# Plain float32 instead of a split for the y steps of the second token tile of batch 0

## The chip, the cores and the metric

One Trainium2 chip, one core. The metric is the device time of one launch in microseconds (us): lower is better. The kernel before takes 1445.43 us (median of three runs, 1445.27 to 1445.69).

## The reference, cut to what matters

```python
p_packed = sm_attn(p, k, v)                 # 32 packed queries read all 576 keys
out = sm_attn(q, p_packed, p_packed)        # every query reads the 32 packed rows
x = out.transpose(0, 2, 1, 3).reshape(4608, 512)
h = x @ w_in                                # first MLP, 512 -> 2048
g = where(h >= 1, h, where(h <= -1, 0, (h + 1)**2 / 4))
y = g @ w_out                               # 2048 -> 512
h2 = y @ w2_in
return (h2 * sigmoid(h2)) @ w2_out          # second MLP
```

There are 8 batches of 576 tokens. Everything is float32.

## The kernel before, in words

The kernel runs attention and the first MLP batch by batch, then the second MLP over all tokens. The change lies in the first MLP of batch 0, within the first 140 us of the program.

**Steps.** A batch has 576 tokens, in two token tiles t = 0 and 1 of 288, and the 2048 hidden features are 16 blocks m of 128. A step is one tile and one block. Batch 0 runs in four groups of eight: steps 0 to 7 are tile 0 with blocks 0 to 7, steps 8 to 15 tile 1 with blocks 0 to 7, steps 16 to 23 tile 0 with blocks 8 to 15, steps 24 to 31 tile 1 with blocks 8 to 15. From batch 1 on a tile runs through all 16 blocks.

**What a step does.** `a_h` (L652, matmuls L661) computes the 128 x 288 block of h: six matmuls into one of the four banks of `ps_h`. `a_relu` (L671) makes u = (relu(h/2 + 1/2)) squared on ACT, two instructions (L676, L677). `a_max` (L680, DVE L682) finishes u and frees the bank. Then a split step makes g, a pair of fp32r numbers: `a_hi` (ACT cast, L686) rounds u, `a_lo` (L689, L692) subtracts. `a_y` (L694) multiplies g by the block's output weights into four accumulators of `ps_a`, one for each 128 columns of y: for each, three fp32r matmuls (high x high, high x low, low x high; L707), so twelve in a step. A plain step has no g: `a_y` multiplies u by plain float32 weights, one matmul for each accumulator (L703), which the trace records as two. `plain(s)` (L668) says which steps these are: before, steps 0 to 7.

**Low parts.** `a_lo` runs on POOL for blocks 0 to 7 of batch 0 and on DVE elsewhere. At the end of each group of eight, ACT and DVE copy the four accumulators to `ysb` (L716, L719), or DVE adds them to what is there (L714), and the next group's first y step may overwrite an accumulator only when it has been copied.

**Weights.** The weights arrive as float64 words. `conv_a` (ACT, L147) and `conv_b` (two DVE instructions, L153 and L154) turn a block into float32. `conv_c` (L191) splits it: ACT casts the high part (L194) and POOL subtracts (L196). Blocks 0 to 7 are kept plain for steps 0 to 7 and split for steps 8 to 15 and later batches.

**Buffers.** `big` has 37 buffers of 4 KB per partition. u has two homes: plain steps take one of the four buffers of tag `g`, which g tiles take too, all others one of three buffers of tag `u`. The buffer of a u is free when its last reader is through: the low part for a split step, the y matmuls for a plain one.

**Order.** All engines work through their own queue in program order. The queue's order is that of numbers: each job has a key, by default worked out from the step it belongs to (`hi`, `lo`, `co` and so on at the end of the function), and a table `START` by hand gives the key of most jobs of batch 0: relu17 (the relu of step 17) has 13.81, y13 14.6, relu19 15.373, y15 16.603, lo17 16.632. Jobs are sorted by key once; a job that needs something later simply waits in its queue. Besides the steps, the queues hold batch 1's attention (`front`, `back8`) and the products `wp` of packed rows with input weights (`wp_out`, L136 and L137).

Of the kernel before, what the change touches and what calls it, by code (L numbers as in the profile page):

```python
# [8 lines left out]
F32 = mybir.dt.float32  # L9
# [4 lines left out]
ALU = mybir.AluOpType  # L14
# [58 lines left out]
def attention_then_two_mlps(ctx: ExitStack, tc: tile.TileContext, kT, vv, qT, pT, w_in, w_out, w2_in, w2_out, out):  # L73


    nc = tc.nc
    B, P, NJ, S = kT.shape
# [7 lines left out]
    KF = DFF // P  # L85
# [4 lines left out]
    FW = 512  # L90
# [11 lines left out]
    big = ctx.enter_context(tc.tile_pool(name="big", bufs=37))  # L102
# [46 lines left out]
    def to_f32_end(dst, raw):  # L149


        words = words_of(raw)
        nc.vector.tensor_single_scalar(words[:, :, 0], words[:, :, 0], 29, op=ALU.logical_shift_right)  # L153
        nc.vector.scalar_tensor_tensor(  # L154
            dst.bitcast(U32), words[:, :, 1], 3, words[:, :, 0], op0=ALU.logical_shift_left, op1=ALU.bitwise_or
        )

    raw_t, part_t, w_t = {}, {}, {}
# [23 lines left out]

    def conv_b(key):
        if key[0] == "o" and key[1] < KF // 2:
            w = big.tile([P, FW], F32, tag="big", name="w")
        else:
            w = cv.tile([P, FW], F32, tag="w", name="w")
        to_f32_end(w, raw_t.pop(key))
        w_t[key] = w
# [459 lines left out]
    h_ps, u_t, g_t, acc, y_t = {}, {}, {}, {}, {}  # L649
# [16 lines left out]


    def plain(s):  # L668
        return s[:2] == (0, 0) and s[2] < KF // 2

    def a_relu(s):  # L671
        if plain(s):
            u = wk.tile([P, HB], F32, tag="g", name="u", bufs=4)
        else:
            u = a2_p.tile([P, HB], F32, tag="u", name="u", bufs=3)
        nc.scalar.activation(u, h_ps[s][:, :HB], AF.Relu, bias=half, scale=0.5)  # L676
        nc.scalar.activation(u, u, AF.Square)  # L677
        u_t[s] = u
# [9 lines left out]

    def a_lo(s):  # L689
        g = g_t[s]  # L690
        eng = nc.gpsimd if s[0] == 0 and s[2] < KF // 2 else nc.vector
        eng.tensor_tensor(g[:, 1], u_t.pop(s), g[:, 0].bitcast(F32), op=ALU.subtract)  # L692

    def a_y(s):  # L694
        b, t, m = s
        first, last = m in starts[b], m + 1 in starts[b] or m == KF - 1
        if first:
            acc["y"] = [ps_a.tile([P, 512], F32, tag="acc", name="ps_y") for _ in range(KD)]
        w = w_t["o", m]
        g = u_t.pop(s) if plain(s) else g_t.pop(s)  # L700
        for d in range(KD):
            if plain(s):
                nc.tensor.matmul(  # L703
                    acc["y"][d][:, :HB], w[:, d * P:(d + 1) * P], g, start=first, stop=last
                )
            for n, (i, k) in enumerate(() if plain(s) else PASSES):
                nc.tensor.matmul(  # L707
                    acc["y"][d][:, :HB], w[:, i, d * P:(d + 1) * P], g[:, k],
                    start=(first and n == 0), stop=(last and n == 2),
                )  # L710
            if last:
                if ("y", d // 2) in part_t:
                    ysb = part_t["y", d // 2]
                    nc.vector.tensor_tensor(ysb[:, d % 2], acc["y"][d][:, :HB], ysb[:, d % 2], op=ALU.add)  # L714
                elif d % 2:
                    nc.scalar.copy(ysb[:, 1], acc["y"][d][:, :HB])  # L716
                else:
                    ysb = wk.tile([P, 2, HB], F32, tag="ysb", name="ysb", bufs=2)
                    nc.vector.tensor_copy(ysb[:, 0], acc["y"][d][:, :HB])  # L719
                if d % 2:  # L720
                    part_t.pop(("y", d // 2), None)
                    nc.sync.dma_start(y_dram[:, d - 1:d + 1, t, b * HB:(b + 1) * HB], ysb)
# [226 lines left out]
    def ev(key, fn, *args):  # L949
        events.append((key, len(events), fn, args))  # L950
# [4 lines left out]
    def job(name, key, fn, *args):  # L955
        ev(START.get(name, key), fn, *args)
# [6 lines left out]
    with tc.manual_schedule():  # L963
# [36 lines left out]
        def c(letter, key):  # L1000
            if letter == "a":
                seq("a" + kn(key), conv_a, key)
            elif letter == "b":
                seq("b" + kn(key), conv_in if key[0] == "in" else conv_b, key)
            else:
                seq("c" + kn(key), conv_c, key)
# [56 lines left out]
        for i in (2, 3):  # L1063
            for k in range(6):
                job(f"S{i}.{k}", -2 + k + 0.6, s2j[i][k][0])
        job("bo2", -LA + 0.62, conv_b, ("o", 2))
        job("ao3", -LA + 1.62, conv_a, ("o", 3))
        job("bo3", -LA + 2.62, conv_b, ("o", 3))
        T_F1 = -1
        for i, key in enumerate(ins[KD:2 * KD]):  # L1070
# [16 lines left out]
        for m in range(4, KF):  # L1087
            n = m - 3 if m < KF // 2 else m + G['oraw'] + 1
            key = ("o", m)
# [3 lines left out]
            if m >= KF // 2:  # L1093
                job(f"co{m}", n + 2 + .66, conv_c, key)
        for m in range(KF // 2):
            job(f"co{m}", KF // 2 + m - 2.4, conv_c, ("o", m))
        job("part0", 2 * KF // 2 + KF // 2 - 5 + .67, load_part, 0, 0)
        job("part1", 2 * KF - 5 + .67, load_part, 0, 1)

# [41 lines left out]
        for p in range(NPR):  # L1141
            for kind, n in (("i2", G['ai'] + G['ad'] * p), ("o2", G['ai'] + G['ad'] * p + 12)):
                for x in range(2):
                    key = (kind, 2 * p + x)
# [59 lines left out]
        for i, (kind, step) in enumerate(steps):  # L1204
            if kind == "a":
                h = late.get(i, i - LA)
                hi = min(h + 2, i - 1)
                lo = min(h + 3, i - 1)
                if i < 20:
                    job(f"h{i}", h + 0.3, a_h, step)  # L1210
                    job(f"relu{i}", h + 1 + 0.31, a_relu, step)
                    if not plain(step):
                        job(f"hi{i}", hi + (0.32 if hi > h + 1 else 0.35), a_hi, step)
                        job(f"lo{i}", lo + (0.33 if lo > hi else 0.36), a_lo, step)
                    job(f"max{i}", h + 1 + 0.34, a_max, step)
                    job(f"y{i}", i + 0.9, a_y, step)
                else:
                    when(h, 0, a_h, step)
                    when(h + 1, 1, a_relu, step)
                    when(hi, 2 if hi > h + 1 else 5, a_hi, step)  # L1220
                    when(lo, 3 if lo > hi else 6, a_lo, step)
                    when(h + 1, 4, a_max, step)
                    when(i, 9, a_y, step)
# [42 lines left out]
```

## Time and profile before

| what | value |
|---|---|
| median of three runs | 1445.43 us |
| the profiled execution | 1445.66 us |
| its span, first to last instruction | 1443.6 us |
| PE busy | 1429.9 us, 99% of the span |
| DVE, ACT, POOL busy | 951.3, 766.2 and 74.8 us |
| granted TensorE clock | full in all 40 slices |
| PE on the chain that ended last | 90% |
| DVE on it | 5% |

PE is TensorE's matmuls, DVE VectorE, ACT ScalarE, POOL GpSimd. In a timeline row stand the start in us from the span's start, the time that the merged instructions took, engine, line, operation, tiles, shapes and count, and in brackets idle time before the row with what ended it. The time of a matmul row overlaps the next row, so a step's cost is read as the distance between starts. The line numbers are those of the kernel before.

### The profile page before, as it was taken

The page shows a single profiled execution, that of the slowest core. Times are in us where ns is not written, and L with a number is a line of the kernel's source. Part 1 is how long each engine was busy: PE and PEld are TensorE (multiplying, and loading weights), DVE is VectorE, ACT ScalarE, POOL GpSimd, SP SyncE. Part 2 cuts the span into 40 slices and gives each one's busy share as a digit, 9 for nine tenths or more (in the row PEclk, how much of TensorE's full clock was granted, in tenths as well). Part 3 has the DMA queues.
Part 4 walks back from the last instruction along what each step waited for, and adds up shares of the span by engine and source line. Part 5 has one row for each costly group of instructions (what it writes and reads, how often), then busy time and mean ns, then how long its engine had stood idle before and what let it go on. Part 6 is the DMA issues. An engine that isn't in the chain of part 4 may idle for free.

```text
span 1443.6 us, 26352 instructions
## 1 busy us (share of the span) xinstructions
PE 1429.9 (99%) x9812; PEld 1280.5 (89%) x9812; DVE 951.3 (66%) x1711; ACT 766.2 (53%) x1536; POOL 74.8 (5%) x116
## 2 busy tenths in 40 slices
PE   8999999999999999999999999999999999999999
PEld 7778989989899898999998888888888889999998
DVE  5788586675867758577736775477646764774664
ACT  4776667676676767766653452334423541362342
POOL 0250000000000000000000000000000000000000
PEclk9999999999999999999999999999999999999999
DMA  9654545646464555545337677866787678888886
GB/s 346 230 199 131 195 163 185 230 156 222 153 223 162 187 179 190 192 156 185 105 93 241 193 208 222 267 191 193 230 258 195 193 222 281 260 269 285 253 252 223
DMA packets 178639, 300.32 MB, mean 208 GB/s; under 512 B 28624, under 2 KB 76752, under 8 KB 178512
## 3 DMA queue, kind: packets, MB, share of 16 engines
q1 hardware_dynamic: 167760, 264.36, 58.2%
q0 software_dynamic: 9344, 33.04, 6.7%
q8 instruction: 78, 1.28, 0.4%
q10 hardware_dynamic: 1408, 1.25, 0.3%
q14 instruction: 49, 0.40, 0.1%
HBM read 244.97 MB, written 53.61 MB: 207 GB/s over the span
## 4 chain that ended last, share of the span: by engine, by line
PE 90%; DVE 5%; DMA 2%; issue 1%; ACT 1%; POOL 0%; DVEq 0%; ACTq 0%; POOLq 0%
PE ps_y L707 25%; PE ps_o L904 24%; PE ps_h L842 22%; PE ps_h L661 12%; PE ps_wp L573 2%; PE ps_y L703 1%; PE ps_pp L364 1%; DMA qt<-qT 1%; DMA raw<-w_in 1%; DVE g L692 1%; DMA va<-vv 1%; PE ps_s L270 0%; DVE u L682 0%; DVE gt L887 0%; DVE w L154 0%
## 5 line engine op out<-in xcount | busy, mean ns | idle before, releaser
L707 PE MATMUL ps_y<-g,w_o 128*128 128x288 f32 x2976 | 443.8, 298 | 3.0 <-DVE g L692 1.8
L707 PEld LDWEIGHTS ps_y<-g,w_o 128*128 128x128 f32 x2976 | 407.7, 188 | 35.1 <-ACT u L676 10.1
L842 PE MATMUL ps_h<-y,a2r 128*128 128x512 f32 (+1 forms) x1680 | 347.7, 367 | 0.4 <-DVE p L868 0.2
L904 PE MATMUL ps_o<-g,a2r 128*128 128x512 f32 (+1 forms) x1680 | 345.8, 367 | 0.0
L842 PEld LDWEIGHTS ps_h<-y,a2r 128*128 128x128 f32 x1680 | 305.2, 188 | 40.9 <-DVE p L868 1.8
L904 PEld LDWEIGHTS ps_o<-g,a2r 128*128 128x128 f32 x1680 | 305.7, 188 | 39.2
L661 PE MATMUL ps_h<-a,wp 128*128 128x288 f32 x1536 | 246.2, 296 | 1.1 <-DVE u L682 0.4
L682 DVE SCALAR_TENSOR_TENSOR u<-ps_h,u 128x288 f32<-128x288 f32 x256 | 116.1, 455 | 160.2 <-ACT u L677 159.8
L661 PEld LDWEIGHTS ps_h<-a,wp 128*128 128x128 f32 x1536 | 217.3, 188 | 4.4 <-issue 1.6
L676 ACT ACTIVATE u<-ps_h,half 128x288 f32<-128x288 f32 x256 | 128.2, 501 | 171.4 <-PE ps_h L661 147.5
L677 ACT ACTIVATE u<-u 128x288 f32<-128x288 f32 x256 | 113.8, 445 | 8.1
L692 DVE TENSOR_TENSOR g<-u,g 128x288 fp32r<-128x288 f32 x240 | 109.6, 457 | 1.7 <-ACT g L686 1.7
L686 ACT CAST g<-u 128x288 fp32r<-128x288 f32 x248 | 103.5, 417 | 0.2 <-PE ps_y L703 0.2
L800 DVE TENSOR_TENSOR g<-gs,g 128x1024 fp32r<-128x1024 f32 (+1 forms) x80 | 86.7, 1112 | 7.4 <-ACT g L799 7.4
L863 ACT COPY p<-ps_h 128x512 f32<-128x512 f32 (+1 forms) x40 | 21.8, 545 | 124.1 <-PE ps_h L842 116.2
L799 ACT CAST g<-gs 128x1024 fp32r<-128x1024 f32 (+1 forms) x80 | 73.9, 962 | 8.6 <-PE ps_o L904 5.8
L868 DVE TENSOR_TENSOR p<-ps_h,p 128x512 f32<-128x512 f32 (+1 forms) x80 | 50.2, 633 | 39.9 <-PE ps_h L842 39.4
L800 DVE TENSOR_TENSOR g<-gt,g 128x1024 fp32r<-128x1024 f32 (+1 forms) x60 | 64.5, 1112 | 6.8 <-ACT g L799 6.8
L878 ACT ACTIVATE gs<-u 128x512 f32<-128x512 f32 (+1 forms) x40 | 23.6, 589 | 82.6 <-DVE u L868 82.6
L878 ACT ACTIVATE gs<-ps_h 128x512 f32<-128x512 f32 (+1 forms) x40 | 22.3, 556 | 63.3 <-PE ps_h L842 63.3
L799 ACT CAST g<-gt 128x1024 fp32r<-128x1024 f32 (+1 forms) x60 | 53.8, 963 | 0.5 <-PE ps_o L904 0.5
L645 POOL DMA_DIRECT2D win<-win_dram x48 | 25.5, 532 | 515.1 <-DVE g L692 113.2
(142 smaller groups left out, 1145.0 us busy)
## 6 DMA issues: line engine op xcount, KB each, us to landing
a2r<-a_dram SPq DMA_DIRECT2D x280, 256.0 KB, 3.0
a2r<-o_dram SPq DMA_DIRECT2D x280, 256.0 KB, 3.0
win<-win_dram POOLq DMA_DIRECT2D x48, 512.0 KB, 4.3
raw<-w_in SPq DMA_DIRECT2D x32, 512.0 KB, 7.4
raw<-w_out SPq DMA_DIRECT2D x32, 512.0 KB, 6.3
a_dram<-a2w SPq DMA_DIRECT2D x56, 256.0 KB, 2.8
o_dram<-a2w SPq DMA_DIRECT2D x56, 256.0 KB, 2.7
y_dram<-ysb SPq DMA_DIRECT2D x36, 288.0 KB, 2.5
```

What stands on the lines that cost most here:

```text
L661: nc.tensor.matmul(ps[:, :HB], w[:, i, o:o + P], a2[:, k, g, :], start=(n == 0), stop=(n == 3 * NG - 1))
L676: nc.scalar.activation(u, h_ps[s][:, :HB], AF.Relu, bias=half, scale=0.5)
L677: nc.scalar.activation(u, u, AF.Square)
L682: nc.vector.scalar_tensor_tensor(u, h_ps.pop(s)[:, :HB], 1.0, u, op0=ALU.max, op1=ALU.min)
L686: nc.scalar.copy(g[:, 0], u_t[s])
L692: eng.tensor_tensor(g[:, 1], u_t.pop(s), g[:, 0].bitcast(F32), op=ALU.subtract)
L707: nc.tensor.matmul(acc["y"][d][:, :HB], w[:, i, d * P:(d + 1) * P], g[:, k], start=(first and n == 0), stop=(last and n == 2),)
L799: nc.scalar.copy(hi, src)
L800: nc.vector.tensor_tensor(lo, src, hi.bitcast(F32), op=ALU.subtract)
L842: nc.tensor.matmul(ps, w[:, x, a * P:(a + 1) * P], b_t[i, j][k][:, a], start=(n == 0 and j in FIRST), stop=(n == 3 * KH - 1), skip_group_c ...
L868: nc.vector.tensor_tensor(t, bk[*key, b][:, :w], x, op=ALU.add)
L904: nc.tensor.matmul(ps, w[:, x, d * P:(d + 1) * P], g[k][:, p % 2], start=(p == 0 and n == 0 and j in FIRST), stop=(p == NPR - 1 and n == 2 ...
```

## The change

Three things. Steps 8 to 15 become plain too, so all sixteen y steps of batch 0 with blocks 0 to 7 are. The eight splits of blocks 0 to 7 (`co0` to `co7`) move from keys 5.6 to 12.6 to keys 22.6 to 29.6, ahead of batch 1, which needs them from step 32 on. The plain weights, which must now live longer, share buffers in pairs. u of a plain step takes tag `g` only for even blocks, and tag `u` for odd ones. The low parts on POOL are gone, since no split step of batch 0 has a block below 8 any more.

```diff
     def conv_b(key):
         if key[0] == "o" and key[1] < KF // 2:
-            w = big.tile([P, FW], F32, tag="big", name="w")
+            pair = "pair", key[1] // 2
+            if pair not in w_t:
+                w_t[pair] = big.tile([P, 2, FW], F32, tag="big", name="w")
+            w = w_t[pair][:, key[1] % 2]
...
     def plain(s):
-        return s[:2] == (0, 0) and s[2] < KF // 2
+        return s[0] == 0 and s[2] < KF // 2
 
     def a_relu(s):
-        if plain(s):
+        if plain(s) and s[2] % 2 == 0:
             u = wk.tile([P, HB], F32, tag="g", name="u", bufs=4)
         else:
             u = a2_p.tile([P, HB], F32, tag="u", name="u", bufs=3)
...
     def a_lo(s):
         g = g_t[s]
-        eng = nc.gpsimd if s[0] == 0 and s[2] < KF // 2 else nc.vector
-        eng.tensor_tensor(g[:, 1], u_t.pop(s), g[:, 0].bitcast(F32), op=ALU.subtract)
+        nc.vector.tensor_tensor(g[:, 1], u_t.pop(s), g[:, 0].bitcast(F32), op=ALU.subtract)
...
         for m in range(KF // 2):
-            job(f"co{m}", KF // 2 + m - 2.4, conv_c, ("o", m))
+            job(f"co{m}", 22.6 + m, conv_c, ("o", m))
```

In `START` the sixteen entries hi8 to hi15 and lo8 to lo15 are gone, all others keep their numbers. So PE's, DVE's and SP's queues keep their order, and in ACT's the eight casts of g and the eight casts of `co0` to `co7` leave the place where they stood. Line numbers from L186 on differ by a few: L661 and L676 are the same, L703 becomes L702, L707 L706, L136 L133, L716 L715.

The first place is ACT's queue around steps 16 to 19. The u written by relu17 is u_1069 before and u_978 after, that of relu19 is u_1121 before and u_1021 after; the casts to g are high parts, w_o are the weight splits, wp the products. Before:

```order
L676 ACTIVATE u_1069<-ps_h_1026,half_86 128x288
...
L147 ACTIVATE raw_842<-raw_842 128x512
L136 CAST wp_1_3_1077<-ps_wp_957 128x512
L686 CAST g_1080<-u_1033 128x288
...
L676 ACTIVATE u_1118<-ps_h_1101,half_86 128x288
...
L676 ACTIVATE u_1121<-ps_h_1110,half_86 128x288
...
L194 CAST w_o_10_1138<-w_1066 128x512
L147 ACTIVATE raw_1057<-raw_1057 128x512
L686 CAST g_1165<-u_1118 128x288
L716 COPY ysb_1170<-ps_y_805 128x288
```

Between relu19 and the copies of y15 stand a weight split, a conversion and hi18 (g_1165). After the change, where u_821 and u_871 are the u of steps 13 and 15, u_868 that of step 14 and u_955 that of step 16:

```order
L676 ACTIVATE u_821<-ps_h_797,half_86 128x288
...
L676 ACTIVATE u_868<-ps_h_840,half_86 128x288
...
L676 ACTIVATE u_871<-ps_h_849,half_86 128x288
...
L676 ACTIVATE u_955<-ps_h_876,half_86 128x288
...
L676 ACTIVATE u_978<-ps_h_948,half_86 128x288
...
L686 CAST g_988<-u_955 128x288
...
L676 ACTIVATE u_1018<-ps_h_1001,half_86 128x288
...
L676 ACTIVATE u_1021<-ps_h_1010,half_86 128x288
...
L194 CAST w_o_10_1030<-w_975 128x512
L144 ACTIVATE raw_966<-raw_966 128x512
L686 CAST g_1057<-u_1018 128x288
L715 COPY ysb_1060<-ps_y_779 128x288
```

The relus keep their order; of these u, steps 13, 15, 16, 17, 18 and 19 (all but u_868) are now in tag `u` with its three buffers.

The second place is PE's queue from y13 to y16 after the change:

```order
L702 MATMUL ps_y_781<-u_821,w_560 128x288
L661 MATMUL ps_h_1001<-a2_357,wp_0_2_806 128x288 x3
...
L661 MATMUL ps_h_1010<-a2_357,wp_0_2_806 128x288 x3
...
L702 MATMUL ps_y_778<-u_868,w_623 128x288
...
L661 MATMUL ps_h_1038<-a2_357,wp_0_3_990 128x288 x3
...
L702 MATMUL ps_y_781<-u_871,w_623 128x288
L661 MATMUL ps_h_1076<-a2_357,wp_0_3_990 128x288 x3
...
L706 MATMUL ps_y_1100<-g_988,w_o_8_937 128x288 x3
```

The last matmul of y13 reads u_821, then come h18, h19, y14, h20, y15 (u_871), h21 and y16, as before; y13 to y15 read u and plain w where they read g and w_o.

The third place is ACT's queue from step 25 on after the change, where the first three moved casts now stand, each behind a high part:

```order
L686 CAST g<-u 128x288
L194 CAST w_o_1321<-w 128x512
L524 ACTIVATE e_1214<-e_1214 128x512
L676 ACTIVATE u<-ps_h,half 128x288
L677 ACTIVATE u<-u 128x288
L686 CAST g<-u 128x288
L194 CAST w_o_1356<-w 128x512
```

Each cast is followed by a subtraction on POOL, whose queue had nothing at this point before.

## Rows read from the trace of the kernel before

**Rows 1.** Waits of PE, 66 to 130 us: us in total, times, longest.
```profile
PE ps_y L707 <- DVE g L692: 1.6, 1, 1.6
PE ps_y L707 <- POOL g L692: 1.2, 1, 1.2
PE ps_s2e L495 <- DVE u L682: 1.0, 1, 1.0
PE ps_wp L561 <- DVE u L682: 0.5, 1, 0.5
```
**Rows 2.** Windows: length, busy PE, PEld, DVE, ACT, POOL, then clock, DMA share, GB/s.
```profile
66.50:96.80 30.30, 28.48 (x270) 23.07 (x269) 22.46 (x40) 23.18 (x50) 17.06 (x14) 1.00 0.61 215
96.80:112.60 15.80, 13.07 (x121) 10.30 (x120) 14.46 (x24) 11.34 (x25) 6.61 (x5) 1.00 0.45 143
112.60:131.00 18.40, 18.40 (x152) 17.36 (x146) 17.86 (x46) 12.07 (x30) 0.00 (x0) 1.00 0.37 114
131.00:150.00 19.00, 19.00 (x173) 17.00 (x172) 9.85 (x24) 11.35 (x28) 0.00 (x0) 1.00 0.72 229
```
**Rows 3.** Timeline of PE: two plain y steps, then two split ones with h between.
```profile
59.91 4.04 PE L703 MATMUL ps_y<-u,w 128*128 128x288 f32 x16
...
64.58 2.10 PE L703 MATMUL ps_y<-u,w 128*128 128x288 f32 x8
...
115.13 1.77 PE L707 MATMUL ps_y<-g,w_o 128*128 128x288 f32 x12
116.74 0.96 PE L661 MATMUL ps_h<-a,wp 128*128 128x288 f32 x6
117.54 1.75 PE L707 MATMUL ps_y<-g,w_o 128*128 128x288 f32 x12
```
**Rows 4.** Timeline of PE: y11's restart, y13, h18 and h19, y15, h21, y18's restart.
```profile
78.34 1.75 PE L707 MATMUL ps_y<-g,w_o 128*128 128x288 f32 x11 [1.20 <-POOL g L692]
...
87.68 1.87 PE L707 MATMUL ps_y<-g,w_o 128*128 128x288 f32 x12
89.46 2.26 PE L661 MATMUL ps_h<-a,wp 128*128 128x288 f32 x12
...
95.05 1.88 PE L707 MATMUL ps_y<-g,w_o 128*128 128x288 f32 x12
96.77 0.96 PE L661 MATMUL ps_h<-a,wp 128*128 128x288 f32 x6
...
102.60 1.75 PE L707 MATMUL ps_y<-g,w_o 128*128 128x288 f32 x11 [1.57 <-DVE g L692]
```
**Rows 5.** Timeline of ACT: relu17, relu19, hi18, the last copy of y15.
```profile
87.87 0.50 ACT L676 ACTIVATE u<-ps_h,half 128x288 f32<-128x288 f32 x1 [0.98 <-POOL g L692]
...
92.37 0.49 ACT L676 ACTIVATE u<-ps_h,half 128x288 f32<-128x288 f32 x1
...
94.35 0.42 ACT L686 CAST g<-u 128x288 fp32r<-128x288 f32 x1
...
96.97 0.40 ACT L716 COPY ysb<-ps_y 128x288 f32<-128x288 f32 x1 [0.42 <-PE ps_y L707]
```
**Rows 6.** Timeline of DVE: max17, lo18, max27.
```profile
88.95 0.46 DVE L682 SCALAR_TENSOR_TENSOR u<-ps_h,u 128x288 f32<-128x288 f32 x1 [0.56 <-ACT u L677]
...
101.05 1.50 DVE L692 TENSOR_TENSOR g<-u,g 128x288 fp32r<-128x288 f32 x1
...
124.30 0.45 DVE L682 SCALAR_TENSOR_TENSOR u<-ps_h,u 128x288 f32<-128x288 f32 x1
```
**Rows 7.** Timeline of POOL: one weight split's subtraction.
```profile
100.95 1.27 POOL L196 TENSOR_TENSOR w_o<-w,w_o 128x512 fp32r<-128x512 f32 x1 [0.26 <-ACT w_o L194]
```
**Rows 8.** Groups of DVE's low parts, 40 to 112 us, then 130 to 400 us.
```profile
L692 DVE TENSOR_TENSOR g<-u,g 128x288 fp32r<-128x288 f32 x6 | 4.8, 802 | 0.0
...
L692 DVE TENSOR_TENSOR g<-u,g 128x288 fp32r<-128x288 f32 x99 | 44.4, 448 | 0.0
```
**Rows 9.** Timeline of PE: h29, which needs the bank that max27 frees.
```profile
125.12 0.96 PE L661 MATMUL ps_h<-a,wp 128*128 128x288 f32 x6
```

29 rows, old and new, of the table START are left out of this document.

## The prediction

> **What bounds the kernel now.** I read the page first: PE is busy 99% of the span at the full granted clock and makes up 90% of the chain that ended last. So time is gained or lost only where PE runs another number of passes, or where it stands still. Next I asked for the waits of PE in the stretch that the change touches. From 66 to 130 us PE stood still in five places, four of them worth a word [rows 1]: 1.2 us for lo11 on POOL, 0.5 us for max15, 1.6 us for lo18 on DVE and 1.0 us for a bank that max22 frees. Then the windows [rows 2] show who is near the limit, stage by stage. Before 97 us no engine is full but PE. From 97 to 113 us DVE is busy 14.46 of 15.80 us. From 113 to 131 us PE has no idle time, and DVE is busy 17.86 of 18.40: two engines full side by side, DVE without reserve. From 131 us on DVE falls to half (9.85 of 19.00) and PE sets the pace alone. After that PE never waits for anything worth naming, so what PE loses in batch 0 is lost for good; nothing later gives it back. Last I read the timelines of PE, ACT and DVE around y13 to y18 [rows 4 to 6].
>
> **The sum, against the profiled execution's own 1445.66 us** (span 1443.6; the median of the runs, 1445.43, is 0.23 lower).
>
> *1. Eight split steps become plain.* Two plain steps and one h of six matmuls run from 59.91 to 64.58 us, 4.67 us; without the h, which is 0.80 us (116.74 to 117.54), that is 1.93 us a step. A split step is 1.61 us (115.13 to 116.74) [rows 3]. I take 0.35 us a step, as a little of the 1.93 may be the change from one kind of matmul to the other (0.31 to 0.36). Eight steps: +2.8 us, bounds 2.5 to 2.9. PE is the bound here, so all of it counts. The row shows a plain matmul at 1.93/1.61 of three split ones. The Trainium skill (FP8 and Floating Point Precision, TensorE Precision Notes) says that true float32 makes four passes through the array; four passes for three would be 1.61 x 4/3 = 2.15 us a step and +4.3 us in all. The row is below that, so I stay with the row.
>
> *2. Stalls that go.* y11 no longer waits for a low part on POOL: 1.2 us [rows 1, 4]. max15 comes earlier, because DVE no longer shares its time with POOL's low parts and splits: 0.5 us. With the restart of the pipeline after each I take -1.9 us, bounds -1.9 to -1.2.
>
> *3. relu17 gets a new master.* This is what the diff hides in one line. The u of an odd plain step now sits in tag `u`, which has three buffers. When relu17 comes up in ACT's queue, the three are held by the u of steps 13, 15 and 16. The first to come free is that of step 13, and it is free only when y13, a PE matmul, is through. Before, relu17 ran at 87.87 us [rows 5], 1.6 us ahead of y13's end at 89.46 [rows 4], and max17 freed its bank at 88.95 + 0.46 = 89.41 [rows 6], just in time for h18. Now relu17 can start only at y13's end, and from there to the end of max17 it takes what it took before: 89.41 - 87.87 = 1.54 us. h18 needs that bank, so PE stands still for about 1.5 us, while behind relu17 on ACT the conversion, the casts of wp and hi16 move back too. A wait that h19 had in the same place (h18 and h19 took 2.26 us, where six such matmuls take 0.96 and six more 0.80 [rows 3, 4]) is partly swallowed. +1.4 us, bounds 0.5 to 2.2.
>
> *4. relu19 waits for y15.* It takes the next buffer to come free: that of step 15, as y15 (key 16.603) stands ahead of lo17 (16.632). Before, relu19 started at 92.37 us, and relu19, its square, a weight split, a conversion and hi18 were through at 94.35 + 0.42 = 94.77, all under y14, h20, wp and y15 on PE, which ended at 96.77 [rows 4, 5]. Now these 2.4 us of ACT work start when y15 ends. Queued behind them on ACT are the two copies of y15's accumulators, a conversion, relu20, a split and two casts of wp; on DVE max19 is late, and behind it stand a conversion, two more copies and lo17. Who waits: h21 for the bank of max19, y16 for the four copies, and relu20 for lo17. All this leads to lo18, for which PE waited already: y18 restarted at 102.60 us, 5.83 us after y15's end [rows 4]. That stall grows by the delay: at least 2.4 us less what may hide, with lo17 in DVE's queue behind a conversion some 0.6 us more. +3.0 us, bounds 1.5 to 4.0 (the upper end with one more POOL subtraction of 1.27 us [rows 7] in the way). Beyond lo18 DVE is full until 131 us [rows 2], so nothing is caught up.
>
> *5. The eight splits in their new place.* ACT has room: 6.3 of the 18.40 us are idle [rows 2], and the five or six casts that fall there would fit even at 1 us each. POOL is empty there, and the SP queue keeps its order; its loads for batch 2 come after the splits. The cost is on DVE. lo18 took 1.50 us at 101.05 instead of 0.45 while POOL subtracted from 100.95 for 1.27 us [rows 6 to 8]: an operation of DVE with two inputs in SBUF stood still until POOL was done. The mean of lows says the same, 802 ns where POOL worked and 448 ns where it did not [rows 8]. Five or six of the eight splits fall into 113 to 131 us, where DVE has 0.5 us left, the others where it has time. Slack: h29 starts 0.37 us after max27 has freed its bank (124.30 + 0.45 against 125.12) [rows 6, 9]. Not all of DVE's work there has two inputs in SBUF, and one that begins just before POOL does is not held up; I take 0.4 us for each of five, the mean excess of a low part beside POOL (802 - 448 ns), less the slack: +1.5 us, bounds 0 to 4.0. The rule behind it is in the Trainium skill (SBUF — State Buffer, Who interferes with whom): a DVE instruction with two SBUF inputs and a GpSimd instruction that reads SBUF shut each other out for the whole instruction. The trace agrees (1.50 us); where every split met such an instruction it would be rival C.
>
> The plain weights in pairs take four `big` buffers for eight and free room; they cost nothing, since the loads of raw weights were not what ACT or PE waited for here. The eight casts to g and eight low parts that go from ACT and POOL lie before 91 us, where only the stalls of part 2 hung on them.
>
> Sum: 2.8 - 1.9 + 1.4 + 3.0 + 1.5 = **+6.8 us**, 1452.5 us against the profiled execution and **1452.2 us** against the median.
>
> **Rivals.**
>
> *A, on the other side: the buffers come free in time and the relief of DVE pays.* If relu19's buffer were freed by lo16 or lo17 (which the order of keys decides: the point is whether y15 stands ahead of lo17), parts 3 and 4 would be 0, and DVE, rid of POOL's company before 91 us, might reach lo18 and max22 in time: -1.6 - 1.0 - 0.2 more. 2.8 - 1.9 - 2.8 = -1.9 us, 1443.5 us. For it speaks that DVE and ACT lose work before 91 us; against it that DVE had idle gaps before 97 us anyway, so it was not behind from there, and that the stall at y18 follows from what comes after y15's end.
>
> *B, only PE's price.* The waits of 3 and 4 are real but PE has enough queued to cover them, and the splits find gaps: 2.8 - 1.9 = +0.9 us, 1446.3 us. Against it: h18 and h21 need banks that exactly these relus free.
>
> *C, the lock takes all.* Six splits each cost DVE the full 1.27 us, 7.6 us less 0.4 of slack, on top of 5.3 from parts 1 to 4: +12.5 us, 1457.9 us.
>
> That the change does not do what it says is no case: PE's queue has the plain matmuls, and the casts stand in their new place.
>
> **How the numbers follow.** My forecast, with its waits in any strength inside the bounds, has 0.72; A 0.07, B 0.11, C 0.10. The sum of lower bounds is 2.5 - 1.9 + 0.5 + 1.5 + 0 = 2.6 us (1448.0), that of upper bounds 2.9 - 1.2 + 2.2 + 4.0 + 4.0 = 11.9 us (1457.3). The range 1446.2 to 1456.2 takes in B and the forecast but for its upper end, and leaves out A and C, under 0.2 in all. About 0.2%, 2.9 us, is what a measurement of this kernel can tell from no change. Slower by more (over 1448.3): forecast and C, 0.82. Within: B and most of A, 0.15. Faster by more (under 1442.5): 0.03.
>
> **What the profile after would show.** Right: 128 records of the plain line where 64 stood; no wait of PE on POOL near 77 us; relu17 idle until y13's end, relu19 idle until y15's end, each released by PE; PE idle before h18 (about 1.4 us) and before h21, released by DVE L682; y18's restart some 8 to 9 us after y15's end instead of 5.8; in the eight subtractions' time low parts of over 1 us, and idle of PE released by DVE. Wrong: PE without idle time between y13 and y16, or a stretch from 113 us on that is as long as before with POOL's subtractions in it (then part 5 is 0).

## The result, and the profile after

The changed kernel takes 1454.3 us (median of six runs, 1453.68 to 1456.8), the kernel before 1445.45 us beside it: ratio 1.0063, 95% interval 1.0053 to 1.0074. That is 8.85 us slower; the forecast was 6.8. The profiled execution of the changed kernel took 1455.8 us, its span 1454.0, 10.4 more than before. The time scatters: in a second series (below) the unaltered changed kernel took 1455.94 us, and three of its eleven executions lie above the 1456.2 at which the predicted range ends.

First the three largest waits of PE from 66 to 160 us (us in total, times, longest), which answer to [rows 1]:

```profile
PE ps_y L706 <- DVE g L691: 3.1, 2, 2.9
PE ps_h L661 <- DVE u L682: 3.1, 2, 1.6
PE ps_y L706 <- DVE ysb L713: 1.4, 1, 1.4
```

The waits of before for POOL (1.2), at wp (0.5) and at s2e (1.0) are gone. Two of 1.6 us each for a bank of `ps_h` are new, the one for lo18 has grown from 1.6 to 2.9 us, and one of 1.4 us for the sums of the y halves is new. PE's timeline says where they are: y13, h18, h19, y14, then y15, h21, y16 with y17, y18's restart, and the starts of y20, y24 and y28.

```profile
87.36 2.11 PE L702 MATMUL ps_y<-u,w 128*128 128x288 f32 x8
91.02 1.06 PE L661 MATMUL ps_h<-a,wp 128*128 128x288 f32 x6 [1.56 <-DVE u L682]
92.27 1.21 PE L661 MATMUL ps_h<-a,wp 128*128 128x288 f32 x6 [0.20 <-DVE wp L134]
93.27 3.68 PE L702 MATMUL ps_y<-u,w 128*128 128x288 f32 x8
...
98.69 2.21 PE L702 MATMUL ps_y<-u,w 128*128 128x288 f32 x8
102.45 1.06 PE L661 MATMUL ps_h<-a,wp 128*128 128x288 f32 x6 [1.56 <-DVE u L682]
103.67 3.99 PE L706 MATMUL ps_y<-g,w_o 128*128 128x288 f32 x25 [0.16 <-ACT ysb L715]
110.52 3.01 PE L706 MATMUL ps_y<-g,w_o 128*128 128x288 f32 x11 [2.86 <-DVE g L691]
...
120.59 1.89 PE L706 MATMUL ps_y<-g,w_o 128*128 128x288 f32 x12
...
132.86 1.82 PE L706 MATMUL ps_y<-g,w_o 128*128 128x288 f32 x12 [1.40 <-DVE ysb L713]
...
144.62 1.85 PE L706 MATMUL ps_y<-g,w_o 128*128 128x288 f32 x12
```

In the timeline of the kernel before the same three steps 20, 24 and 28 start here:

```profile
112.64 1.86 PE L707 MATMUL ps_y<-g,w_o 128*128 128x288 f32 x12
...
123.43 1.86 PE L707 MATMUL ps_y<-g,w_o 128*128 128x288 f32 x12
...
134.22 1.86 PE L707 MATMUL ps_y<-g,w_o 128*128 128x288 f32 x12
```

So the kernel is 7.95 us behind at y20, 9.43 at y24 and 10.40 at y28, as much as the whole span. Nothing is caught up or lost later. From y15's end (102.45 - 1.56 = 100.89 us) to y18's restart it takes 9.63 us; before, 5.83 [rows 4].

The timeline of ACT shows relu17, relu19 and relu20 of the changed kernel, to be read against [rows 5]:

```profile
89.50 0.50 ACT L676 ACTIVATE u<-ps_h,half 128x288 f32<-128x288 f32 x1 [7.21 <-PE ps_y L702]
...
100.93 0.50 ACT L676 ACTIVATE u<-ps_h,half 128x288 f32<-128x288 f32 x1 [6.05 <-PE ps_y L702]
...
105.56 0.50 ACT L676 ACTIVATE u<-ps_h,half 128x288 f32<-128x288 f32 x1 [1.05 <-DVE g L691]
```

relu17 stood 7.2 us and relu19 6.1 us, both released by a plain y matmul of PE: y13 and y15. DVE's timeline goes on from there (max19, a conversion, lo17, lo18, then a product of batch 1's attention and the sums of the y halves), against [rows 6]:

```profile
101.94 0.46 DVE L682 SCALAR_TENSOR_TENSOR u<-ps_h,u 128x288 f32<-128x288 f32 x1 [6.57 <-ACT u L677]
...
103.10 1.33 DVE L151 SCALAR_TENSOR_TENSOR w<-raw 128x512 uint32<-128x512 uint32 x1 [0.37 <-ACT raw L144]
...
105.08 0.44 DVE L691 TENSOR_TENSOR g<-u,g 128x288 fp32r<-128x288 f32 x1
...
109.04 1.43 DVE L691 TENSOR_TENSOR g<-u,g 128x288 fp32r<-128x288 f32 x1
...
130.01 1.82 DVE L534 TENSOR_TENSOR e<-e,r 128x512 f32<-128x512 f32 x1
...
132.26 1.54 DVE L713 TENSOR_TENSOR ysb<-ps_y,ysb 128x288 f32<-128x288 f32 x4
```

and POOL's beside lo18 and beside L534, against [rows 7]:

```profile
108.88 1.27 POOL L196 TENSOR_TENSOR w_o<-w,w_o 128x512 fp32r<-128x512 f32 x1 [0.21 <-ACT w_o L194]
...
130.00 1.28 POOL L196 TENSOR_TENSOR w_o<-w,w_o 128x512 fp32r<-128x512 f32 x1 [0.92 <-ACT w_o L194]
```

One thing in the PE rows stands in no term of the prediction. y14's eight records took 3.68 us and y13's eight 2.11; y18's eleven took 3.01 and before 1.75 [rows 4]. The windows of those two stretches show the clock (length, busy PE, PEld, DVE, ACT, POOL, granted clock, DMA share, GB/s):

```profile
93.20:96.50 3.30, 3.30 (x9) 2.44 (x8) 1.05 (x4) 0.95 (x3) 0.00 (x0) 0.51 0.00 0
...
110.50:113.40 2.90, 2.88 (x12) 2.88 (x13) 2.66 (x6) 1.50 (x4) 0.00 (x0) 0.50 0.86 349
```

Twice, behind a wait of 1.56 and one of 2.86 us, PE ran at half its full clock, 1.2 GHz in place of 2.4.

### The profile page after: what moved, and what is told of

Read it like the earlier page. It is cut to its first block, busy times and chain, and to the rows that moved or that the text cites. A ratio compares the mean times of both kernels' runs of the same rounds, so it can differ in the third digit from the quotient of the medians.

```text
span 1454.0 us, 26236 instructions
## 1 busy us (share of the span) xinstructions
PE 1436.8 (99%) x9780; PEld 1282.3 (88%) x9780; DVE 948.1 (65%) x1711; ACT 763.2 (52%) x1528; POOL 65.2 (4%) x108
## 3 DMA queue, kind: packets, MB, share of 16 engines
q8 instruction: 78, 1.28, 0.4%
## 4 chain that ended last, share of the span: by engine, by line
PE 90%; DVE 6%; DMA 2%; ACT 1%; issue 1%; POOL 0%; DVEq 0%; ACTq 0%; POOLq 0%
PE ps_y L706 24%; PE ps_o L903 24%; PE ps_h L841 23%; PE ps_h L661 12%; PE ps_y L702 2%; PE ps_wp L573 2%; PE ps_pp L364 1%; DVE g L691 1%; DMA qt<-qT 1%; DMA raw<-w_in 1%; DMA va<-vv 1%; DVE u L682 1%; PE ps_s L270 0%; PE ps_wp L561 0%; DVE wp L134 0%
## 5 line engine op out<-in xcount | busy, mean ns | idle before, releaser
L706 PE MATMUL ps_y<-g,w_o 128*128 128x288 f32 x2880 | 431.3, 299 | 5.0 <-DVE g L691 3.4
L706 PEld LDWEIGHTS ps_y<-g,w_o 128*128 128x128 f32 x2880 | 395.8, 189 | 36.0 <-ACT u L676 10.1
L661 PE MATMUL ps_h<-a,wp 128*128 128x288 f32 x1536 | 247.4, 297 | 4.1 <-DVE u L682 3.6
L682 DVE SCALAR_TENSOR_TENSOR u<-ps_h,u 128x288 f32<-128x288 f32 x256 | 116.0, 455 | 170.3 <-ACT u L677 169.9
L676 ACT ACTIVATE u<-ps_h,half 128x288 f32<-128x288 f32 x256 | 128.1, 501 | 188.3 <-PE ps_h L661 151.4
L661 PEld LDWEIGHTS ps_h<-a,wp 128*128 128x128 f32 x1536 | 217.7, 188 | 8.8 <-DVE u L682 5.5
L686 ACT CAST g<-u 128x288 fp32r<-128x288 f32 x240 | 100.1, 417 | 0.0
```

Source lines behind the costliest of these rows:

```text
L661: nc.tensor.matmul(ps[:, :HB], w[:, i, o:o + P], a2[:, k, g, :], start=(n == 0), stop=(n == 3 * NG - 1))
L682: nc.vector.scalar_tensor_tensor(u, h_ps.pop(s)[:, :HB], 1.0, u, op0=ALU.max, op1=ALU.min)
L686: nc.scalar.copy(g[:, 0], u_t[s])
L706: nc.tensor.matmul(acc["y"][d][:, :HB], w[:, i, d * P:(d + 1) * P], g[:, k], start=(first and n == 0), stop=(last and n == 2),)
```

## The experiments

All medians stand beside the kernel before, which took 1445.47 to 1445.61 us in these comparisons.

**Undo parts 3 and 4.** One more plain u goes to tag `g`, that of step 15; then three buffers of tag `u` are enough for relu17 and relu19.

```diff
-        if plain(s) and s[2] % 2 == 0:
+        if plain(s) and (s[2] % 2 == 0 or s == (0, 1, 7)):
```

> One choice is undone: the u of step 15 goes to tag g again. Then relu17 takes the buffer of step 11 and relu19 that of step 16, and neither waits for a y. Theory (masters of relu17 and relu19, parts 3 and 4): PE's 1.6 us before h18 and 1.6 us before h21 are gone, y18 restarts about 6 us after the end of y15 instead of 10.0, and the time falls by 1.4 + 4.2 = 5.6 us to about 1448.7. First rival (the plain matmuls cost four passes, part 1 is 4.3 and the waits are covered): the time stays within 1.5 us of 1454.3. Second rival (the low part of step 18 is late for other reasons, DVE and POOL): only the wait at h18 and h21 goes, and the time falls to about 1452.

Measured: 1448.12 us (1447.12 to 1449.63, 11 runs), ratio to before 1.0018 (1.0010 to 1.0027). The waits at h18 and h21 are gone; y15's end and y18's restart in PE's timeline of this run are

```profile
96.71 1.17 PE L661 MATMUL ps_h<-a,wp 128*128 128x288 f32 x6
...
102.67 1.75 PE L706 MATMUL ps_y<-g,w_o 128*128 128x288 f32 x11 [1.47 <-DVE g L691]
```

5.96 us, as before the change. So both rivals fall: what the two relus wait for is worth 1454.3 - 1448.12 = 6.2 us of the 8.85.

**Undo part 3 alone.** The u of step 13 goes to tag `g`; relu19 still takes the buffer of step 15.

```diff
-        if plain(s) and s[2] % 2 == 0:
+        if plain(s) and (s[2] % 2 == 0 or s == (0, 1, 5)):
```

> Part 3 alone is undone: the u of step 13 goes to tag g, so relu17 waits for no y, while relu19 still takes the buffer of step 15 and waits for y15. Theory: PE no longer stands before h18 (1.6 us), it still stands before h21, and y18 still restarts some 10 us after the end of y15; time 1454.3 - 1.4 = 1452.9. Rival (relu17's delay was the cause of the whole late chain up to lo18): the time falls as far as in the run with step 15 in tag g, to about 1448.7. Rival (what is saved at h18 is given back at h21): within 0.4 us of 1454.3.

Measured: 1451.98 us (1451.57 to 1453.25, 5 runs), ratio 1.0047 (1.0034 to 1.0059). Its PE timeline at the same two places:

```profile
98.48 1.06 PE L661 MATMUL ps_h<-a,wp 128*128 128x288 f32 x6 [1.56 <-DVE u L682]
...
106.55 1.75 PE L706 MATMUL ps_y<-g,w_o 128*128 128x288 f32 x11 [1.75 <-DVE g L691]
```

No wait at h18; h21 waits as in the changed kernel, and from y15's end (96.92) to y18 it takes 9.63 us, to the hundredth what the changed kernel needs. So the long way to lo18 belongs to relu19 alone: part 4 is 1451.98 - 1448.12 = 3.9 us, part 3 is 1454.3 - 1451.98 = 2.3 us. The 2.3 hangs on which executions of the changed kernel are taken: the median of all eleven is 1455.2 and would give 3.2, that of the five with the highest mean granted clock (last section) is 1454.06 and gives 2.1.

**Undo part 5 alone.** The eight splits five steps later.

```diff
-            job(f"co{m}", 22.6 + m, conv_c, ("o", m))
+            job(f"co{m}", 27.6 + m, conv_c, ("o", m))
```

> Part 5 alone is undone: the eight moved splits go five steps further, to 27.6 to 34.6, into the stretch where DVE is half idle. Theory (POOL's subtractions hold up DVE where it is full): PE's wait of 1.4 us for the sums of the y halves and the small ones at the lows of steps 24 to 31 go, h18, h21 and lo18 stay; from the start of y20 to that of y28 it takes 21.6 us again instead of 24.0; time 1454.3 - 2.4 = 1451.9. Rival (the splits are hidden anyway and DVE is late there because all of it came late): no change, 1454.3.

Measured: 1451.01 to 1454.89 us in five executions, their median 1451.71, 2.6 us below the changed kernel; a sixth took 6300 us and is left out. It is the one with the profile, and its matmuls took several times as long (those of L706 1061 ns in the mean, 299 in the changed kernel), so that neither the way from y20 to y28 nor the wait for the sums of the y halves can be compared: whether that wait goes is seen only in the next run.

**Both repairs.**

```diff
+        if plain(s) and (s[2] % 2 == 0 or s == (0, 1, 7)):
+            job(f"co{m}", 27.6 + m, conv_c, ("o", m))
```

> Both: the u of step 15 in tag g and the splits five steps later. What is left of the change is eight plain steps. Theory (the parts add up): 1454.3 - 5.6 - 2.4 = 1446.3, 0.9 us above the kernel before, that is the price of the plain steps (2.8) less the two stalls that went (1.9). Rival (four passes for three, part 1 is 4.3): 1447.8. Rival (DVE, now without the lows of the early steps, also catches lo18): 1443.5 to 1444.7, faster than before.

Measured: 1445.59 us (1444.7 to 1445.77, 11 runs), ratio 0.9999 (0.9990 to 1.0008): no difference from the kernel before. h21, y18, y20, y24 and y28 in PE's timeline:

```profile
96.45 1.18 PE L661 MATMUL ps_h<-a,wp 128*128 128x288 f32 x6
...
102.42 1.73 PE L706 MATMUL ps_y<-g,w_o 128*128 128x288 f32 x11 [1.47 <-DVE g L691]
...
112.45 1.86 PE L706 MATMUL ps_y<-g,w_o 128*128 128x288 f32 x12
...
123.24 1.85 PE L706 MATMUL ps_y<-g,w_o 128*128 128x288 f32 x12
...
134.03 1.85 PE L706 MATMUL ps_y<-g,w_o 128*128 128x288 f32 x12
```

At each step it stands 0.19 us ahead of the kernel before. With the two repairs eight plain steps cost as much as the stalls that they end; the splits (part 5) are worth 1448.12 - 1445.59 = 2.5 us. The rival of DVE catching lo18 falls: 1.47 us of wait are still there.

**Is it POOL or ACT's casts?** The split cut in two, the subtraction later than the cast.

```diff
         nc.scalar.copy(t[:, 0], w)
+        if key[0] == "o" and key[1] < KF // 2:
+            w_t["s", key[1]] = w, t
...
+            job(f"cd{m}", 27.6 + m, conv_d, m)
```

> As the run with the u of step 15 in tag g (1448.1), but each of the eight moved splits is cut in two: ACT's cast stays at 22.6 to 29.6, POOL's subtraction goes to 27.6 to 34.6. Theory (POOL's subtraction holds up DVE: beside it L534 of step 24 took 1.82 us instead of 0.69 and L532 0.85 instead of 0.17): the wait of 1.4 us at step 24 goes and the time is that of the run with the whole splits moved, 1445.6. Rival (the eight casts crowd ACT, and relu and hi of steps 22 to 30 come late): the time stays at 1448.1. In between, both would share it.

Measured: 1447.87 us (1447.45 to 1448.5, 11 runs). By its expectation that is the rival's number, but the trace says that the run did not ask the question: the third subtraction began at 122.22 us, 0.7 us after its cast began, as in the run that it should differ from (122.09). POOL has nothing else to do there, so a later key moves nothing; only the cast, at its place in ACT's queue, sets when it starts. A miss.

**The same question, POOL not reading.** On the first run's kernel:

```diff
+        if key[0] == "o" and key[1] < KF // 2:
+            nc.gpsimd.memset(t[:, 1].bitcast(F32), 0.0)
```

> As the run with the u of step 15 in tag g (1448.1), but POOL writes zeros into the low half of the eight moved splits in place of the subtraction, so the low parts of the first eight blocks of output weights are left out from batch 1 on. POOL's instruction stands in the same place of its queue, started by the same cast of ACT, and reads nothing from SBUF; ACT's casts stay. Theory (a subtraction of POOL, with its reads from SBUF, holds up DVE's operations with SBUF inputs): L534 of step 24 takes 0.69 us again in place of 1.82, PE's wait of 1.4 us before y24 goes, the time is 1445.6. Rival (ACT's casts or POOL's place in itself make the low parts late): the wait stays, 1448.1.

Measured: 1445.38 us (1444.65 to 1446.03, 11 runs), ratio 0.9999 (0.9990 to 1.0008). POOL's memsets didn't stay in their place: without the cast to wait for, all eight ran from 110.02 us on, 3.79 us together. The casts stayed: those of the first three splits stand at 116.22, 118.62 and 121.00 us, within 0.4 us of the run with subtractions, and they cost nothing. In the first run L534 of step 24 and the subtraction both begin at 122.09 us and take 1.82 and 1.28 us, as their rows at 130 us in the changed kernel do. Here the same operation of DVE (three lines further down in this file) has POOL idle beside it:

```profile
121.03 0.69 DVE L537 TENSOR_TENSOR e<-e,r 128x512 f32<-128x512 f32 x1
```

The 1.13 us between them are most of PE's 1.4 us before y24. That it is not any work of POOL shows where the memsets ran: beside these, which write and read nothing, DVE took 0.69 us for the same kind of operation and 0.42 us for a low part,

```profile
111.87 0.69 DVE L523 TENSOR_TENSOR e<-e,m 128x512 f32<-128x512 f32 x1
...
112.72 0.42 DVE L694 TENSOR_TENSOR g<-u,g 128x288 fp32r<-128x288 f32 x1
```

```profile
110.02 3.79 POOL L197 MEMSET w_o<- 128x512 f32 x8
```

where lo18 beside a subtraction took 1.43. The time came as in the theory, and in this profile PE has no wait before y24; that the reading makes the difference is concluded from these two kinds of POOL instruction alone.

**The clock.** Twenty small matmuls of zeros in PE's queue between y13 and h18, and the changed kernel once more beside it.

```diff
+        if s == (0, 0, 10):
+            for i in range(20):
+                d = i % KD
+                nc.tensor.matmul(
+                    acc["y"][d][:, :64], w_t["o", 5][:, d * P:(d + 1) * P], zero, start=False, stop=False
+                )
```

> The changed kernel with twenty small plain matmuls (64 columns, of zeros, added to the open sums of y14) between y13 and h18, where PE otherwise stands still for 1.6 us. Theory (PE's clock falls after it stood still, which in the profiled execution of the changed kernel made the matmuls of y14 start every 480 ns instead of every 243): y14 runs at 243 ns in the profile, the time is at most that of the changed kernel (1454.3), and no execution lies above 1455.5, while the changed kernel itself reached 1456.8. Rival (the slow y14 has another cause, such as what ACT and DVE do beside it): the 480 ns stay, the scatter stays. If the matmuls are longer than the wait, the time rises by what they exceed it, up to 0.5 us.

> The changed kernel itself, unaltered, beside the run with the fill. Theory: median 1453.7 to 1455.5 with a scatter of 2 to 3 us, and in the profile the matmuls of y14 or of y18 may or may not start at half the rate; where they do not, the span is 2 to 3 us shorter than the 1454.0 of the first profile. Rival (half the rate belongs to every execution): 480 ns at y14 again and a span within 0.5 us of 1454.0.

Measured: with the fill 1456.15 us (1455.87 to 1458.25, 5 runs); the changed kernel again 1455.94 (1454.06 to 1457.02, 5 runs). The fill was too long, 4.39 us (89.26 to 93.65) for a wait of 1.56, so its time says nothing on the clock, and its expectation (at most 1454.3 us, none above 1455.5) is missed. In its profile the clock fell behind the wait of 2.90 us for lo18 (0.73 from 110.5 to 113.4 us). y14 ran at full clock behind the fill, but so it did in the second profile of the unaltered kernel, where h18 waited the same 1.56 us; there the low clock stood elsewhere, behind a wait of 2.10 us for a DMA:

```profile
32.50:36.60 4.10, 3.17 (x39) 3.08 (x40) 2.27 (x5) 1.64 (x4) 0.00 (x0) 0.61 1.05 371
...
93.20:96.50 3.30, 3.09 (x17) 2.48 (x16) 2.06 (x6) 2.29 (x5) 0.00 (x0) 1.00 0.00 0
```

So a low clock at y14 is not part of every execution, and the rival falls. The theory's own sign failed as well: though y14 and y18 ran at full clock, the span was not 2 to 3 us shorter but 1454.8, and the median of 1455.94 lies above the 1453.7 to 1455.5 that were expected. In this execution y8 already started 1.3 us later than in the first profile (70.16 against 68.83 us).

**A version that beats both?** On the run with both repairs, conversions and splits of blocks 10 to 15 moved up into the stretch before 97 us, the conversions (`ao`, `bo`) ahead of each split with it; of the new keys some are shown. First trial:

```diff
-    "co10": 15.509648, "bo11": 16.66, "co11": 17.521621, "co12": 17.603301, "co13": 19.535, "co14": 20.16,
+    "co10": 13.4, "bo11": 13.3342, "co11": 13.45, "co12": 14.45, "co13": 15.38, "co14": 15.71,
```

> The run with both repairs (1445.6) and, beyond it, the conversions and splits of blocks 10 to 15 of the output weights moved up from keys 13.7 to 20.2 to keys 13.3 to 16.6, into the stretch before 97 us, where DVE is busy 18 of 31 us and ACT 19 of 31. Theory (the waits that are left from 97 to 112 us, 1.5 us for lo18 on DVE, 1.0 us for the bank of max22 and 0.2 us, come from this work on DVE and from POOL's subtractions beside it): they go, 1445.6 - 2.7 = 1442.9. Rival (they come from the chain relu20, lo17, lo18 itself): 1445 to 1445.6. Rival on the other side (the moved work delays the relus of steps 17 to 20, and PE stands still before h18 to h21): over 1446.

Measured: 1445.04 us (1444.31 to 1445.69, 11 runs), ratio 0.9996 (0.9987 to 1.0005). The waits of PE:

```profile
PE ps_h L661 <- DVE wp L134: 1.4, 1, 1.4
PE ps_y L706 <- DVE g L691: 0.3, 1, 0.3
PE ps_y L706 <- DVE ysb L718: 0.3, 1, 0.3
```

Both waits that it aimed at are almost gone, but the cast of co12 on ACT waits for bo12 on DVE, and the casts of wp stand behind it. Second trial, with co12 behind relu19, co14 behind lo18 and block 15 where it was:

```diff
+    "co10": 13.1, "bo11": 13.06, "co11": 13.15, "bo12": 15.3762, "co12": 15.3763, "co13": 16.61, "co14": 18.05,
```

> The run with both repairs (1445.6), with conversions and splits of blocks 10 to 14 moved up, placed so that no relu, cast of wp or copy of the y sums stands behind a wait: in the first trial of this kind PE's waits at 102 and 109 us shrank from 2.7 to 0.6 us, but a cast of wp that stood behind a split cost 1.4 us before h19. Theory: 1445.6 - 2.0 to 2.7 = 1442.9 to 1443.6, faster than both kernels. Rival (the work only moves its waits about): 1445 or more.

Measured: 1442.66 us (1442.1 to 1444.01, 11 runs), ratio 0.9980 (0.9972 to 0.9989), 2.8 us faster than the kernel before. In its profile no wait of PE is listed from 66 to 160 us. DVE was the crowded one from 97 to 113 us, as this window of the run with both repairs and then of this one shows:

```profile
97.00:113.00 16.00, 13.36 (x123) 10.54 (x122) 14.59 (x25) 11.56 (x26) 6.59 (x5) 1.00 0.44 141
```

```profile
97.00:113.00 16.00, 16.00 (x145) 13.44 (x144) 13.34 (x26) 11.77 (x27) 4.50 (x3) 1.00 0.43 141
```

**The same on the kernel before**, with lo11 on DVE:

```diff
-        eng = nc.gpsimd if s[0] == 0 and s[2] < KF // 2 else nc.vector
+        eng = nc.gpsimd if s[0] == 0 and s[2] < KF // 2 and s != (0, 1, 3) else nc.vector
```

> The kernel before, with the same conversions and splits moved up as in the run before this, and the low part of step 11 on DVE in place of POOL. Theory (the plain steps aren't needed for it, their price of 2.8 us is saved): 1445.5 - 1.2 - 2.0 to 2.7 = 1441.6 to 1442.3. Rival (before 97 us the kernel before has not the room: DVE is busy 23 of 31 us and ACT 24 of 31 there, POOL's low parts and splits lock DVE on top): 1445 or more, with PE waiting between 84 and 97 us.

Measured: 1447.47 us (1446.15 to 1449.05, 11 runs), ratio 1.0012 (1.0003 to 1.0021). Its waits of PE:

```profile
PE ps_h L661 <- DVE ppt L375: 1.7, 1, 1.7
PE ps_h L661 <- DVE u L682: 1.0, 1, 1.0
PE ps_wp L561 <- DVE u L682: 0.7, 1, 0.7
```

The waits from 97 us on are gone here too, but 3.4 us come up between 84 and 95 us, where the kernel before waits 0.5, and behind the one of 1.7 us the clock fell (0.64 from 88 to 92 us). The window from 76 to 88 us of this run shows DVE full, with POOL's low parts and splits beside it:

```profile
76.00:88.00 12.00, 9.59 (x125) 6.82 (x125) 11.39 (x18) 8.64 (x18) 9.45 (x7) 0.98 0.87 287
```

With the plain steps, and the same work moved up, DVE is busy 9.95 and POOL 5.23 of these 12 us. So in this order of the queues the plain steps pay, once the room that they make before 97 us is used; whether another order would serve the kernel before as well was not tried.

## Why the prediction was right, and where its sizes were off

Its sign and its places held, and so did the mechanism of parts 1 to 4; in part 5 the operations that were held up were not those that it priced. Part 1 stood; the other four were too small, the gain of part 2 by 0.8 us and the three costs by 0.9 to 1.0 each, so that the gain hid a part of what the costs missed. The measured differences, 0.1 + 2.5 + 3.9 + 2.3 = 8.8 us from 1445.5, add up because each begins where the one before ends, which proves nothing; what tests them is part 5 undone alone on the changed kernel, 2.6 us against the 2.5 here.

| term | forecast | measured | from |
|---|---|---|---|
| 1 and 2, plain steps less stalls | +0.9 | +0.1 | both repairs against before |
| 3, relu17 waits for y13 | +1.4 | +2.3 (2.1 to 3.2) | u of step 13 in `g` |
| 4, relu19 waits for y15 | +3.0 | +3.9 | u of 13 against u of 15 in `g` |
| 5, splits in the full stretch | +1.5 | +2.5 | both repairs against u of 15 in `g` |

- **1 and 2.** In the run with both repairs a plain matmul still starts every 243 ns by its records, eight in a step, 1.94 us (85.08 to 87.02), as [rows 3] had it. So the price of 2.8 stands and the stalls that went are worth more, 2.8 - 0.1 = 2.7 us against 1.9. In PE's timeline before stand twelve matmuls of h and the first of y11:

```profile
75.26 1.76 PE L661 MATMUL ps_h<-a,wp 128*128 128x288 f32 x12
76.85 0.29 PE L707 MATMUL ps_y<-g,w_o 128*128 128x288 f32 x1
```

y11 took from 76.85 to the next h at 79.93 us, 3.08 us for a step of 1.6: its wait of 1.2 cost 1.5. And h18 and h19 took 2.26 us [rows 4] where twelve such matmuls take 1.76: a gap of 0.5 us that the prediction put under part 3 and that is gone in the run with both repairs (1.98, behind a plain step, as the twelve at 75.87 us with 1.97). With the 0.5 of max15 these are 2.5 of the 2.7. The Trainium skill (FP8 and Floating Point Precision, TensorE Precision Notes) names four passes for true float32; at the length of a split matmul each, as the prediction works out, that would have been 4.3 us for the plain steps. The trace does not speak against four passes, only against their length: a plain matmul is two records of 243 ns, 486 ns or 122 for each pass, while a split matmul takes 133 ns, so four for three cost 486 / 399 = 1.22, not 1.33.
- **3.** h18 waited 1.56 us, forecast 1.5. What was left out is behind it: 0.20 us more for wp before h19, since the casts of wp stand behind relu17 on ACT, and what PE loses around the two waits: y14 started 93.27 - 90.89 = 2.4 us later than in the run without them, 0.6 more than both, before the clock comes in. That the old wait at h19 would swallow a part was wrong: it was gone already.
- **4.** All steps came as told: relu19 at y15's end, h21 waits for max19, y16 for a copy, relu20 for lo17, lo18 under a POOL subtraction. y18 restarted 9.63 us after y15's end, forecast 8 to 9. The size was near the upper end, where the prediction had put one more POOL subtraction: L151 took 1.33 us beside POOL ahead of lo17, 0.64 more than the next one at 105.97 us without it (0.69).
- **5.** POOL's subtractions hold up DVE as told, but hardly at the low parts. The 802 ns of [rows 8] are no low part beside POOL: of these six two took 1.50 and 1.56 us, beside a subtraction, and four 0.41 to 0.45. The forecast took their mean for five places that it did not look up, so that it came within 1.0 us is in part luck. In the run with the u of step 15 in `g` these of DVE were held up:

```profile
117.77 0.85 DVE L532 TENSOR_SCALAR r<-r 128x16 f32<-128x16 f32 x1
...
128.55 1.62 DVE L555 TENSOR_TENSOR a<-e2t,a 128x288 fp32r<-128x288 f32 x2
...
132.22 0.94 DVE L691 TENSOR_TENSOR g<-u,g 128x288 fp32r<-128x288 f32 x1
```

The first, 0.17 us without POOL, and L534 (1.82 against 0.69) lie in one chain to the sums that y24 waits for, 1.8 us together, and 1.4 of it reached PE. The other two (0.74 and 0.45 without) stand behind y24, where y28 lost another 1.0 us in the changed kernel (10.40 - 9.43); 0.26 of it is a wait for that low part in either run, the rest was not told apart. The Trainium skill (SBUF — State Buffer, Who interferes with whom) has the rule for L534, which reads two tiles, and says that such an instruction does not contend with one of GpSimd that only writes; the product beside the memsets agrees (0.69 us). The same section of the Trainium skill says that a tensor_scalar can enter a mode that uses the shared port, and 0.85 us for L532 agrees; the prediction had counted two inputs alone.
- **Rivals.** A fell with the keys, B is the run with both repairs (1445.6 against 1446.3). C had the right rule with too many collisions.
- **Not in the sum.** The clock, below. In the first profile PE came to s2e so late, at half clock, that its wait of 1.0 us there is gone; in the second it is back.

## What to carry to other kernels

When a tile moves to another pool tag, write down who frees the buffer that each later instruction will get: one line of this diff made two ACT instructions wait for a PE matmul, and that cost more (6.2 us) than all the matmuls that the change added (2.8). A job's key moves work only on an engine that has other work there; on an idle engine what starts the work is its last input. Work saved ahead of a full stretch was worth nothing here until something from that stretch was moved into the room.

## What the runs showed of the hardware

**The clock after a stall.** PE's granted clock fell to half, 1.2 GHz, behind some waits: 1.56 and 2.86 us in the first profile, 2.10 us in the second, and not behind others of the same length in the same program: 1.56 us before h21 in the first, 1.56 before h18 and 2.90 before y18 in the second. Of eleven executions of the changed kernel, the five with a mean granted clock of 0.999 or more took 1453.7 to 1454.5 us, the six with 0.998 or less 1455.2 to 1457.0. In all eleven of the run with both repairs, whose longest wait from 66 us on in batch 0 is 1.5 us, the mean was 1.000 and the times lay within 1.1 us. A half-clock stretch cost up to 1.6 us (y14), and nothing where a later wait covered it: in the run with the u of step 13 in `g`, 25 matmuls of y16 and y17 at clock 0.67 only shortened the wait for lo18 from 2.86 to 1.75 us. That stalls cause it is what all places have in common; the run that was to show it by filling one was too coarse, and so it is not shown.

**Who is held up by POOL's subtraction.** In the run with the u of step 15 in `g` a tensor_scalar of 16 columns was (0.85 us for 0.17), while the reduction beside it (0.67 us) and a transposition (0.70) took their usual time, and so did the finish of u (L682, 0.45 us at 119.93), one of whose two inputs comes from a bank of `ps_h`.
